# Feed-forward weights: split once and stored to scratch in the first row chunk, read back from there in the other three

## The chip, the core and the metric

The kernel runs on one core of a Trainium2 chip. The metric is the device time of one execution in microseconds (us), first to last: the median of three runs before the change is 1343.92 us.

## The reference

The output is a gated sum of two branches over the same 2048 rows of 512 values. Branch A is attention with 32 heads of 16 values that share one key and one value head. Branch B is a feed-forward network of width 1792. A gate per row, from `gate_w`, mixes them.

```python
g = sigmoid((x * gate_w).sum(-1, keepdims=True))
q = (x @ wq) per head; k = x @ wk; v = x @ wv
a = (softmax(q k^T * Dh**-0.5) @ v) over the heads @ wo
b = (silu(x @ w_gate) * (x @ w_up)) @ w_down
return g * a + (1 - g) * b
```

All inputs and the output are float32. Matmuls whose two sides would lose too much in one pass are made of three: each side is split into a rounded part (`h`, for high) and the rest (`l`, for low), and hh, hl and lh products are summed (`three`, L110).

## The kernel before, in words

**Preparation (L590 to L632).** x is loaded and transposed, and its two parts are kept for row chunks 0 and 1 (a chunk is 512 rows, there are four). Those of chunks 2 and 3 are stored to the scratch `x_d` and loaded again later. Keys, values and the gate are made, and the queries of the first 8 heads.

**Main loop (L771 to L815).** The order of every engine is written out by hand. For each head and each 128 keys, PE makes scores (`pss`, L660), ACT takes their exponentials (`pt`, L668; for some tiles DVE first copies half of the scores, L664), and PE sums them with the values (`po`, L680, in `mix`). From the 33rd group of keys on, four groups make one block (`block`, L711), which ends with four `mix` calls. Between the score matmuls, the block feeds matmuls of other jobs (`feed`, `Halves`, `Job.step` with L176): first the queries of the other 24 heads, then the feed-forward network. A job's 12 or 15 products run in two halves of 64 rows each: the low half first, the high half some steps later, after a one-element marker on DVE (`sign`, L403).

**Queries.** `query` (L198) leaves a job's result in `hh`, `hl` and, for the bound on the scores, in `hs` or `ht`; each is stored to the scratch `q_d` from SP (L232), where `load_head` (L640) reads the next head's queries into `qs`. The buffers: 7 for `hh`, 7 for `hl`, 2 each for `hs` and `ht`.

**Feed-forward.** For row chunk m and block f of 128 of the 1792 columns (14 of them), n = 14 m + f counts the steps. For every n there are three weight tiles of 128 x 512: g (`w_gate`), u (`w_up`) and d (`w_down`). In these texts g2 is the tile of `w_gate` for n = 2. `gate_up` makes the hidden values, `down` their product with `w_down`, summed over groups of four or five steps.

**The weights.** `load_w` (L144) calls `load_split` (L134). SP loads 256 KB into a raw buffer (`wraw`, L137; two of them, `WRB`), and GpSimd makes the two parts from it: a cast (L106) and a subtraction (L107). Each part of g and of u has two buffers, each part of d has five. So the splits of g and u for step n + 2 wait until PE has read those of step n. All four chunks need the same weights, so each tile is loaded and split four times. The loads for n = 0 and 1 and of the first five d tiles (L765 to L770) come before the loop; later ones of g and u are issued when a job of step n has ended (L309), those of d two at a time after jobs (L185). SP issues its DMAs in order, and waits at each until its buffer is free and its data is there. Among the weight loads stand the stores of `q_d`, of the attention output (`osb` to `o_d`, L694), and the loads of `qs`.

**Tail (L818 on).** When the attention is done, the remaining jobs run with all 128 rows at once, and `finish` (L432) multiplies the attention output, split by GpSimd from `o_d` (`load_o`, L424), with `wo`.

Of the kernel before, what the change touches and what calls it, by code (L numbers as in the profile page):

```python
# [8 lines left out]
F32 = mybir.dt.float32  # L9
F32R = mybir.dt.float32r  # L10
# [8 lines left out]
P = 128  # L19
S = 2048  # L20
D = 512
# [3 lines left out]
KD = D // P  # L25
NT = S // P
CH = 512
NCH = S // CH
TC = CH // P
NF = F // P  # L30
# [32 lines left out]
def tile_gated_mix(ctx, tc, x, wq, wk, wv, wo, w_gate, w_up, w_down, gate_w, out):  # L63
    nc = tc.nc
    x = x.rearrange("b s d -> (b s) d")
# [3 lines left out]
    dpool = ctx.enter_context(tc.tile_pool(name="dpool", bufs=1, space=DRAM))  # L69
# [5 lines left out]
    o_d = dpool.tile([D, S], F32, name="o_d")  # L75
    a_d = dpool.tile([NCH, P, TC, D], F32, name="a_d")
    x_d = dpool.tile([2, 2, P, KD, CH], F32, name="x_d")
    wq_v = wq.rearrange("(k p) n -> p k n", p=P)

    ident = cpool.tile([P, P], F32, name="ident")  # L80
# [20 lines left out]
    wp = tc.alloc_tile_pool(name="wp", bufs=2)  # L101
# [3 lines left out]
    def split(hi, lo, src, eng=nc.gpsimd, eng_hi=nc.vector):  # L105
        eng_hi.tensor_copy(hi, src)  # L106
        eng.tensor_tensor(lo, src, hi.bitcast(F32), ALU.subtract)  # L107
# [11 lines left out]
    wg_v = w_gate.rearrange("(k p) f -> p k f", p=P)  # L119
    wu_v = w_up.rearrange("(k p) f -> p k f", p=P)  # L120
    W, HT = {}, {}
    ACTS, DEFER, LOADS, HOLD, EVAC, FRESH = [], [], [], [], [], set()

    def run(queue, n):
        for _ in range(min(n, len(queue))):
            queue.pop(0)()
# [7 lines left out]
    def load_split(view, name, bufs, pool=wp):  # L134
        shape = list(view.shape)
        raw = wp.tile(shape, F32, name="wraw", bufs=WRB)
        nc.sync.dma_start(raw, view)  # L137
        hi = pool.tile(shape, F32R, name=name + "h", bufs=bufs)
        lo = pool.tile(shape, F32R, name=name + "l", bufs=bufs)
        split(hi, lo, raw, nc.gpsimd, nc.gpsimd)  # L140
        return hi, lo


    def load_w(nm, n):  # L144
        if n < NCH * NF:
            fs = slice(n % NF * P, (n % NF + 1) * P)
            if nm == "d":
                W[nm, n] = load_split(w_down[fs, :], "wd", 5)
            else:
                W[nm, n] = load_split({"g": wg_v, "u": wu_v}[nm][:, :, fs], "w" + nm, 2)  # L150

    def load_x_again(c):
        if c in ORDER:
# [99 lines left out]
    def gate_up(n, c):  # L253
# [53 lines left out]
        for nm, end in (("g", gate), ("u", up)):  # L307
            r.append(Job(3 * KD, lambda nm=nm: (nm, n) in W and c in XC, project(nm), end))
            r[-1].after.append(lambda nm=nm: load_w(nm, n + 2))  # L309
# [30 lines left out]
    def jobs():  # L340
        late = []
        for m, c in enumerate(ORDER):
            for fs in GROUPS:
                ns = [m * NF + f for f in fs]
                new = [job for n in ns for job in gate_up(n, c)]
                if late:
                    late[-1].after.append(lambda ns=ns: LOADS.extend([lambda n=n: load_w("d", n) for n in ns]))
                if fs[-1] == NF - 1:
                    if m < 2:
                        new[-1].after.append(lambda m=m: load_x_again(ORDER[m + 2]))  # L350
                for j, job in enumerate(new):
                    yield job
                    if late and j:
                        yield late.pop(0)
                yield from late
                late = [down(ns, c, i) for i in range(TC)]
            late[-1].after.append(lambda c=c: store_acc(c))
        yield from late
# [278 lines left out]
    with tc.tile_pool(name="bpool", bufs=2) as bp:  # L637
# [128 lines left out]
        for n in range(2):  # L766
            load_w("g", n)
            load_w("u", n)
        for n in GROUPS[0]:
            load_w("d", n)  # L770
        with tc.manual_schedule():  # L771
            for j in range(2):
                exps(*score(0, j))
            for n in range(BEGIN):
                quota = RATE
                u = 2 * n
# [20 lines left out]
            for k in range(2 * BEGIN // BLOCK, NB):  # L797
                u = BLOCK * k
                if k == 2 * BEGIN // BLOCK:
                    n = u + 6 - (u + 1)  # L800
# [129 lines left out]
```

## Time and profile before

| what | us |
|---|---|
| median of three runs (lowest, highest) | 1343.92 (1343.49, 1346.85) |
| the profiled execution | 1344.01 |
| its span, first to last instruction | 1341.9 |
| GpSimd: CAST and subtraction of the three weights, all 168 tiles | 36.1 + 36.1 + 35.1, 75.4 + 73.2 + 73.1 |
| DMA: moved in all | 107.79 MB, 80 GB/s on the mean |
| HBM | 76.09 MB read, 29.36 MB written |

PE is the matrix engine (PEld its weight loads), DVE the vector engine, ACT the scalar engine, POOL is GpSimd, and SP issues most of the DMAs. A row of the timeline has the start in us, the duration, the engine, the line of the kernel, the operation, what it writes and reads, how many instructions were merged, and in brackets the idle time before it and what ended it. A row of the waits has who waited for whom, the total in us, how often, and the longest. A row of the windows has a stretch, its length, the busy time of PE, PEld, DVE, ACT and POOL with instruction counts, the granted clock of PE as a share, the mean share of the 16 DMA engines, and GB/s.

### The profile page before, as it was taken

What the parts mean: (1) busy time and instruction counts of PE and PEld (TensorE: products, weight loads), DVE (VectorE), ACT (ScalarE), POOL (GpSimd) and SP (SyncE); (2) the same over time, 40 slices, a digit from 0 to 9 for tenths busy, and PEclk for the clock granted to TensorE, in tenths of its full rate; (3) what the DMA queues carried; (4) which work ended last, traced back from release to release, by engine and by line L of the source; (5) the groups of instructions that cost most, each with busy time, mean ns of one, the idle gap of its engine ahead of it and who ended that gap; (6) DMA issues with size and microseconds to landing.
All of it is one profiled execution on the core that took longest, in us unless ns stands there. A gap on an engine that the chain in (4) does not pass through costs nothing. (4 is left out here: it accounts for less than half of the span.)

```text
span 1341.9 us, 26802 instructions
## 1 busy us (share of the span) xinstructions
PE 1328.0 (99%) x10743; PEld 770.4 (57%) x10743; DVE 722.4 (54%) x1221; ACT 1061.6 (79%) x1463; POOL 391.0 (29%) x408
## 2 busy tenths in 40 slices
PE   9999999999999999999999999999999999999997
PEld 7655555555555555555555555555555555555576
DVE  5554565555455555555464555455454565465432
ACT  4578888888888888888888888888888888888400
POOL 6140321152042151152131241142131241333343
PEclk9999999999999999999999999999999999999999
DMA  8455221131122221141131221231121221222154
GB/s 277 142 173 190 65 60 38 35 107 44 44 86 77 78 80 38 35 107 44 52 122 39 82 79 39 57 83 45 52 61 30 81 79 39 74 68 60 44 161 143
DMA packets 101489, 107.79 MB, mean 80 GB/s; under 512 B 9968, under 2 KB 69616, under 8 KB 99696
## 3 DMA queue, kind: packets, MB, share of 16 engines
q1 hardware_dynamic: 99632, 105.81, 27.5%
q8 instruction: 88, 1.44, 0.5%
q10 hardware_dynamic: 1728, 0.20, 0.1%
q14 instruction: 41, 0.34, 0.1%
HBM read 76.09 MB, written 29.36 MB: 79 GB/s over the span
## 5 line engine op out<-in xcount | busy, mean ns | idle before, releaser
L668 ACT ACTIVATE pt<-pss 128x1024 f32<-128x1024 f32 (+1 forms) x1024 | 842.0, 876 | 177.3 <-PE pss L660 146.3
L664 DVE COPY pt<-pss 128x512 f32<-128x512 f32 x354 | 244.8, 692 | 415.6 <-PE pss L660 380.6
L680 PE MATMUL po<-pt,vaug 128*32 128x512 f32 x4096 | 467.6, 595 | 0.0
L660 PE MATMUL pss<-qs,ks 64*128 64x512 f32 x2048 | 403.1, 417 | 1.1 <-ACT pt L668 1.1
L660 PEld LDWEIGHTS pss<-qs,ks 64*128 64x128 f32 x2048 | 193.7, 184 | 218.4 <-ACT pt L668 183.6
L680 PEld LDWEIGHTS po<-pt,vaug 128*32 128x32 f32 x4096 | 119.2, 109 | 260.2 <-issue 255.2
L668 ACT ACTIVATE pt<-pt 128x512 f32<-128x512 f32 x354 | 195.7, 620 | 0.0
L176 PE MATMUL pf<-xh,wgl 64*128 64x512 f32 (+1 forms) x440 | 162.0, 392 | 0.0
L176 PE MATMUL pf<-xh,wgh 64*128 64x512 f32 (+1 forms) x440 | 160.5, 391 | 0.5 <-DVE acc L331 0.2
L176 PE MATMUL pf<-xl,wgh 64*128 64x512 f32 (+1 forms) x440 | 160.2, 390 | 0.0
L176 PE MATMUL pf<-xh,wuh 64*128 64x512 f32 (+1 forms) x440 | 158.4, 391 | 0.7 <-DVE sign L403 0.3
L176 PE MATMUL pf<-xl,wuh 64*128 64x512 f32 (+1 forms) x440 | 158.2, 390 | 0.0
L176 PE MATMUL pf<-xh,wul 64*128 64x512 f32 (+1 forms) x440 | 157.3, 391 | 0.0
L106 POOL CAST wgh<-wraw 128x512 fp32r<-128x512 f32 x56 | 36.1, 644 | 402.6 <-PE pf L176 311.8
L176 PE MATMUL pf<-wdh,hh 64*128 64x512 f32 (+1 forms) x427 | 143.4, 391 | 1.7 <-DVE hh L106 1.7
L176 PE MATMUL pf<-wdh,hl 64*128 64x512 f32 (+1 forms) x427 | 144.1, 390 | 0.0
L176 PE MATMUL pf<-wdl,hh 64*128 64x512 f32 (+1 forms) x427 | 143.4, 390 | 0.0
L689 DVE RECIPROCAL rsb<-rsb 128x128 f32<-128x128 f32 x128 | 117.1, 935 | 10.1 <-issue 8.2
L106 POOL CAST wuh<-wraw 128x512 fp32r<-128x512 f32 x56 | 35.1, 626 | 298.2 <-PE pf L176 245.3
L176 PEld LDWEIGHTS pf<-xh,wgh 64*128 64x128 f32 (+1 forms) x440 | 78.5, 185 | 9.8 <-issue 2.5
L176 PEld LDWEIGHTS pf<-xh,wuh 64*128 64x128 f32 (+1 forms) x440 | 77.3, 185 | 9.3 <-issue 3.7
L176 PEld LDWEIGHTS pf<-xl,wgh 64*128 64x128 f32 (+1 forms) x440 | 78.5, 185 | 6.0
(157 smaller groups left out, 1547.6 us busy)
## 6 DMA issues: line engine op xcount, KB each, us to landing
wraw<-in_B_w_gate_dram SPq DMA_DIRECT2D x56, 256.0 KB
wraw<-in_B_w_up_dram SPq DMA_DIRECT2D x56, 256.0 KB
wraw<-in_B_w_down_dram SPq DMA_DIRECT2D x56, 256.0 KB
qs<-q_d SPq DMA_DIRECT2D x62, 192.0 KB
q_d<-hl SPq DMA_DIRECT2D x18, 256.0 KB
q_d<-hh SPq DMA_DIRECT2D x18, 256.0 KB
o_d<-osb SPq DMA_DIRECT2D x128, 32.0 KB
a_d<-acc SPq DMA_DIRECT2D x4, 1024.0 KB
```

Of the source, the lines that this page charges most:

```text
L106: eng_hi.tensor_copy(hi, src)
L176: ins = nc.tensor.matmul(self.ps, a, b, start=(i == 0 and not half), stop=(last and half != 0))
L660: nc.tensor.matmul(ps[:, b * CH:(b + 1) * CH], ks[rows, kt * P:(kt + 1) * P], QS[h][rows, j, :], start=True, stop=True)
L664: other = nc.vector.tensor_copy(pt[:, CH:], ps[:, CH:]) if half else None
L668: ins = nc.scalar.activation(pt[:, w], ps[:, w], AF.Exp, scale=SCALE)
L680: nc.tensor.matmul(po[c * 2 * DH:(c + 1) * 2 * DH, :], vaug[:, kt, :], pt[:, c * CH:(c + 1) * CH], start=(kt == 0), stop=(kt == NT - 1))
L689: nc.vector.reciprocal(rsb[:, w], rsb[:, w])
```

## The change

In the first row chunk (n under 14) a tile is loaded and split as before. Then both parts are stored to a new scratch tensor `w_d` in HBM, 256 KB each. These stores are not issued at once: they are kept in `KEPT` and issued at the next call of `load_w`, right behind that call's own raw load. In the other three chunks nothing is split: after what is left in `KEPT`, SP loads the two parts from `w_d` into their buffers, with two DMAs of 256 KB. The other uses of `load_split` (`wq`, `wo`) are as before.

```diff
+    w_d = dpool.tile([3, NF, 2, P, D], F32, name="w_d")
...
+    KEPT = []
+
     def load_w(nm, n):
-        if n < NCH * NF:
-            fs = slice(n % NF * P, (n % NF + 1) * P)
-            if nm == "d":
-                W[nm, n] = load_split(w_down[fs, :], "wd", 5)
-            else:
-                W[nm, n] = load_split({"g": wg_v, "u": wu_v}[nm][:, :, fs], "w" + nm, 2)
+        if n >= NCH * NF:
+            return
+        f, bufs = n % NF, 5 if nm == "d" else 2
+        fs = slice(f * P, (f + 1) * P)
+        view = w_down[fs, :] if nm == "d" else {"g": wg_v, "u": wu_v}[nm][:, :, fs]
+        homes = [w_d["gud".index(nm), f, j] for j in range(2)]
+        if nm != "d":
+            homes = [home.rearrange("p (k f) -> p k f", k=KD) for home in homes]
+        if n < NF:
+            W[nm, n] = load_split(view, "w" + nm, bufs)
+            run(KEPT, len(KEPT))
+            KEPT.extend([lambda home=home, part=part: nc.sync.dma_start(home, part.bitcast(F32))
+                         for home, part in zip(homes, W[nm, n])])
+        else:
+            run(KEPT, len(KEPT))
+            W[nm, n] = [wp.tile(list(view.shape), F32R, name="w" + nm + x, bufs=bufs) for x in "hl"]
+            for home, part in zip(homes, W[nm, n]):
+                nc.sync.dma_start(part.bitcast(F32), home)
```

## The prediction

> **What bounds the kernel now.** I read the page's busy times first, then the waits, then the blocks of the attention loop, then DMA by stage.
>
> ```profile
> PE 1328.0 (99%) x10743; PEld 770.4 (57%) x10743; DVE 722.4 (54%) x1221; ACT 1061.6 (79%) x1463; POOL 391.0 (29%) x408
> ```
> ```profile
> POOL wgh L106 <- PE pf L176: 311.8, 39, 34.8
> POOL wuh L106 <- PE pf L176: 245.3, 40, 25.4
> ```
>
> PE is busy for 1328.0 of 1341.9 us; GpSimd, whose work the change takes away, for 391.0. Where GpSimd waits, it mostly waits for PE to let go of a weight buffer: it is ahead of PE, not behind. Busy time of matmuls is modelled, so I tested the bound on the loop's blocks. A block ends with four `mix` calls; it runs from one burst of `po` matmuls to the next.
>
> ```profile
> 392.57 0.64 PE L680 MATMUL po<-pt,vaug 128*32 128x512 f32 x4
> ...
> 1214.56 0.64 PE L680 MATMUL po<-pt,vaug 128*32 128x512 f32 x4
> 1223.95 0.64 PE L680 MATMUL po<-pt,vaug 128*32 128x512 f32 x4
> 1233.31 0.64 PE L680 MATMUL po<-pt,vaug 128*32 128x512 f32 x4
> 1242.72 0.64 PE L680 MATMUL po<-pt,vaug 128*32 128x512 f32 x4
> ```
> ```profile
> 1214.56:1223.95 9.39, 9.39 (x83) 5.36 (x81) 5.40 (x8) 8.46 (x14) 6.90 (x8) 1.00 0.32 90
> 1233.31:1242.72 9.41, 9.41 (x83) 5.38 (x81) 5.99 (x11) 7.96 (x13) 0.00 (x0) 1.00 0.10 28
> ```
>
> In the windows GpSimd's busy time stands before the clock. The block with 6.90 us of splits took 9.39 us, the one with none 9.41. So in the loop PE sets the pace, and the splits cost it next to nothing. From 392.57 to 1242.72 lie 90 blocks, 9.45 us on average.
>
> The one long stage where another resource is full is the beginning, in which the queries are made and stored to `q_d`:
>
> ```profile
> 18.00:28.00 10.00, 10.00 (x58) 8.20 (x57) 5.46 (x8) 4.68 (x9) 8.52 (x10) 1.00 0.95 385
> 46.00:72.00 26.00, 26.00 (x191) 15.23 (x191) 12.64 (x23) 18.62 (x20) 1.91 (x2) 1.00 0.55 200
> 74.00:99.00 25.00, 25.00 (x208) 12.97 (x200) 14.14 (x25) 19.23 (x21) 13.63 (x14) 1.00 0.58 172
> 101.00:136.00 35.00, 34.05 (x272) 17.60 (x269) 16.44 (x32) 29.05 (x32) 2.46 (x3) 1.00 0.60 192
> 390.00:1252.00 862.00, 861.02 (x7267) 484.78 (x7265) 478.39 (x812) 746.81 (x1046) 237.20 (x245) 1.00 0.24 64
> ```
>
> The last two columns are the DMA engines' share and GB/s. From 18 to 28, where `x_d` is stored, the engines are full at 385 GB/s. From 46 to 136 the share never passes 0.60, yet the rate sticks near 200 GB/s: the `q_d` stores seem to fill about half of the engines and leave the others idle. After 390 the share is 0.24.
>
> **The change, part by part.**
>
> *Start: the new stores.* The loads g0, u0, g1, u1, d0 to d4 are all issued inside this stage. Now each is followed by two 256 KB stores, held back until the next load has been issued. So the stores of eight loads, 16 in all, enter SP's queue before the load of g2; those of d4 come just behind it.
>
> ```profile
> 81.03 0.38 SPq L137 DMA_DIRECT2D wraw<-in_B_w_gate_dram  x1
> ...
> 99.14 0.33 SPq L137 DMA_DIRECT2D wraw<-in_B_w_down_dram  x1
> 100.83 0.60 SPq L232 DMA_DIRECT2D q_d<-ht  x1
> 129.66 0.60 SPq L232 DMA_DIRECT2D q_d<-ht  x1
> 130.53 1.03 SPq L137 DMA_DIRECT2D wraw<-in_B_w_gate_dram  x1
> ```
> ```profile
> 78.28 0.69 DVE L222 SCALAR_TENSOR_TENSOR ht<-ht 128x512 fp32r<-128x512 f32 x1
> ...
> 107.72 0.49 DVE L221 TENSOR_SCALAR ht<-hh,kmax 128x512 f32<-128x512 f32 x1 [0.63 <-DMA q_d<-ht]
> ```
> ```profile
> 137.96 0.77 POOL L106 CAST wgh<-wraw 128x512 fp32r<-128x512 f32 x1 [34.24 <-DMA wraw<-in_B_w_gate_dram]
> 138.81 1.60 POOL L107 TENSOR_TENSOR wgl<-wraw,wgh 128x512 fp32r<-128x512 f32 x1
> ```
> ```profile
> 142.42 0.39 PE L176 MATMUL pf<-xh,wgh 64*128 64x512 f32 x1
> ```
>
> This chain has no room. The raw load of g2 was issued at 130.53 and landed at 137.96, its split ended at 140.41, and the first matmul on it (counted in program order) ran at 142.42: 2.0 us of slack. At 107.72 DVE even waited for a `q_d` store, and it was SP that was late: that buffer was filled at 79, and its store was issued at 100.83, behind the raw loads that wait for splits.
>
> The price of a store has two rows. At the `q_d` pace (200 GB/s) 256 KB take 1.31 us, 16 of them 21.0; at the `x_d` pace (385) 0.68, in all 10.9. I take the second: `x_d`'s stores too have all 128 partitions as their outer dimension, `q_d`'s have 8 heads. The Trainium skill, "DMA: Bandwidth & Descriptors", section "Why a DMA increments its semaphore by 16 and not by 1", says that the outermost dimension sets how many of the 16 engines a DMA uses, so 8 for `q_d`; the shares of 0.55 and 0.95 agree, and by that rule the sum is the 10.9.
>
> From this go the pauses in which SP waited for splits. The stage 74 to 99 moved 172 GB/s where 46 to 72 moved 200: 25 x (1 - 172/200) = 3.5 us idle. The splits that made the pauses remain, and each store waits for one, so I credit half, 1.8. SP is then 10.9 - 1.8 = 9.1 us late behind 99, and from there to 130 it issues `q_d` stores at the DMA's pace and catches up nothing. Queued behind it are the `q_d` stores, whose buffers DVE reuses, head 2's `qs`, and g2: whoever stops PE first, the total is the lateness less the smallest slack, 9.1 - 2.0 = **+7.1 us**. Ends: all absorbed by idle engines, 0; the `q_d` price without credit, +19.0.
>
> *First row chunk, later loads.* Each load's stores sit ahead of the raw load after the next. The chunk's tight place is u9:
>
> ```profile
> 277.58 0.38 SPq L137 DMA_DIRECT2D wraw<-in_B_w_up_dram  x1
> ```
> ```profile
> 281.19 1.28 POOL L107 TENSOR_TENSOR wul<-wraw,wuh 128x512 fp32r<-128x512 f32 x1
> ```
> ```profile
> 285.03 0.39 PE L176 MATMUL pf<-xh,wuh 64*128 64x512 f32 x1
> ```
>
> Split done at 282.47, used at 285.03: 2.6 us of slack. Two stores ahead cost two issues of 0.4 and 1.4 us of transfer, 2.2. It just fits; the loads right behind it build up the same delay, so I put **+0.3** (ends 0 and 2).
>
> *Chunks 1 to 3: no split, two direct loads.* 126 splits leave GpSimd, each a cast of 0.61 us and a subtraction of 1.3 (rows below and above): 241 us. A direct load must wait on SP until PE releases the buffer, where the raw load went ahead into `wraw`. Queued behind it on SP are `osb` stores and the next head's `qs`, issued a head ahead. What counts is release to next use:
>
> ```profile
> 1096.19 0.61 POOL L106 CAST wuh<-wraw 128x512 fp32r<-128x512 f32 x1 [5.98 <-PE pf L176]
> ```
> ```profile
> 1105.77 0.39 PE L176 MATMUL pf<-xh,wuh 64*128 64x512 f32 x1
> ```
> ```profile
> 1267.00 7.58 SPq L137 DMA_DIRECT2D wraw<-in_B_w_down_dram  x4
> ```
> ```profile
> 1269.79 0.61 POOL L106 CAST wdh<-wraw 128x512 fp32r<-128x512 f32 x1 [0.49 <-DMA wraw<-in_B_w_down_dram]
> ```
>
> This buffer was free at 1096.2 and used at 1105.8: 9.6 us, about the least of these chunks when I match buffers to matmuls in program order. One 256 KB load lands 2.8 us after its issue; the second adds 0.4 of issue and 0.7 of transfer: 3.9. Six us stay, so **0**; the cover is gone when a pair takes over 9.6 us. The traffic of a chunk doubles, on engines with a share of 0.24. DVE's two-input operations run beside no split any more; on PE I give that **-0.4**, near the two blocks' difference of nothing (ends 0 and -5.0, if all 90 blocks fell from 9.45 to 9.39).
>
> *Tail.* Here PE does wait for DVE, and DVE runs beside the splits of d52 to d55:
>
> ```profile
> 1278.76 0.39 PE L176 MATMUL pf<-wdl,hh 128*128 128x512 f32 x1
> 1278.98 0.39 PE L176 MATMUL pf<-wdh,hl 128*128 128x512 f32 x1
> 1281.03 0.47 PE L176 MATMUL pf<-wdh,hh 128*128 128x512 f32 x1 [1.66 <-DVE hh L106]
> ```
> ```profile
> 1273.11 1.66 DVE L107 TENSOR_TENSOR hl<-ht,hh 128x512 fp32r<-128x512 f32 x1
> ...
> 1275.68 1.49 DVE L692 TENSOR_TENSOR osb<-osb,rsb 128x512 f32<-128x512 f32 x1
> 1277.09 0.68 DVE L266 COPY hs<-pf 128x512 f32<-128x512 f32 x1
> 1278.46 1.17 DVE L284 SCALAR_TENSOR_TENSOR ht<-ht,hs 128x512 f32<-128x512 f32 x1 [0.70 <-ACT ht L276]
> ...
> 1280.92 0.69 DVE L107 TENSOR_TENSOR hl<-ht,hh 128x512 fp32r<-128x512 f32 x1
> ```
>
> The same L107 takes 0.69 us alone and 1.66 beside a split; L692 and L284 are 0.8 and 0.5 over that 0.69, together 2.3 on the way to 1281.03. The step from one of PE's matmuls to the next is 0.22, so its stall is 2.05 - 0.22 = 1.8, and all of it goes: **-1.8**. The eight direct loads (8 x 0.68 = 5.4 us from 1267, and 2.8) are there by about 1275, before PE's stop at 1279.
>
> *Sum.* The profiled execution took 1344.01 us, 0.1 over the median. 1344.0 + 7.1 + 0.3 - 0.4 - 1.8 = 1349.2, so **1349.1** on the median.
>
> **Rivals.**
>
> *The stores are absorbed.* They use the idle half of the engines and the pauses, and g2 is not late. For it: shares of 0.55 to 0.60. Against: 2.0 us of slack and a DVE already waiting. It holds if the lateness stays under 2.0. Time: 1344.0 - 1.8 - 0.4 = 1341.8.
>
> *Direct loads come late.* Doubled transfers meet `osb`, `qs` and the reload of x, and a pair takes over 9.6 us. At 0.4 us each on the some 30 loads with so short a time: +12 on the forecast, 1361. Against: the share of 0.24.
>
> *The splits cost DVE, and so PE, more than the blocks show.* All 90 blocks fall to 9.39 and the start costs nothing: 1344.0 - 1.8 - 5.0 = 1337.2. The mechanism is the stretched L107. The Trainium skill, "SBUF — State Buffer", section "Who interferes with whom", calls the port pair that the two engines share an exclusive lock; the 1.66 beside 0.69 agrees. Against: 9.39 beside 9.41.
>
> *The change moves work that nobody waited for*, in the tail and start too: 1344.
>
> **How the numbers follow.** About 0.3% (4 us) is what a measurement of this kernel can tell from no change. Forecast 0.60, of which 0.08 lie under 1347.9 (a start loss under 6); absorbed 0.22 (0.20 within 0.3%, 0.02 faster); late loads 0.10; DVE 0.05, faster; nothing 0.03. So slower 0.52 + 0.10 = 0.62, within 0.31, faster 0.07. The range, 1341 to 1356, takes in the absorbed case and a start loss of up to 14, and leaves out the late loads, the DVE case and the rest of the `q_d` price, under 0.2.
>
> **What would show it.** After the change GpSimd should be busy some 241 us less, near 150. Right: a PE gap of several us between 107 and 150, DVE waiting for `q_d` stores near 110 for several us instead of 0.63, g2's cast later than 138 beside its use; no gap of 2 us before the last `down` jobs; blocks after 390 unchanged. Wrong: PE without a gap before 150, or waits of PE on DMA in the later chunks.

## The result, and the profile after

The changed kernel takes 1354.0 us (median of six runs, 1352.9 to 1355.7); the kernel before, beside it on the same chip, 1345.4 (six runs, 1343.5 to 1347.1). The ratio is 1.0067, with a 95% interval of 1.0052 to 1.0081: slower, by 0.7%. The profiled execution took 1352.9 us, its span 1350.8, 8.9 more than the span of before.

Busy times on the page of the changed kernel:

```profile
PE 1329.6 (98%) x10743; PEld 770.8 (57%) x10743; DVE 701.8 (52%) x1221; ACT 1061.9 (79%) x1463; POOL 144.3 (11%) x156
```

GpSimd lost 246.7 us of work (391.0 before), and PE is busy for 1.6 us more. Where the time went is read from the same bursts of `po` matmuls in both kernels. Timeline of PE, first before, then after:

```profile
82.64 0.64 PE L680 MATMUL po<-pt,vaug 128*32 128x512 f32 x4
156.25 0.64 PE L680 MATMUL po<-pt,vaug 128*32 128x512 f32 x4
1259.14 0.64 PE L680 MATMUL po<-pt,vaug 128*32 128x512 f32 x4
```
```profile
82.57 0.64 PE L695 MATMUL po<-pt,vaug 128*32 128x512 f32 x4
167.65 0.64 PE L695 MATMUL po<-pt,vaug 128*32 128x512 f32 x4
403.89 0.64 PE L695 MATMUL po<-pt,vaug 128*32 128x512 f32 x4
1270.09 0.64 PE L695 MATMUL po<-pt,vaug 128*32 128x512 f32 x4
```

Up to 82 the two run alike. Between the bursts at 82 and 156 the changed kernel loses 11.5 us, up to the last burst it gains 0.5 back (11.40 to 10.95), and from there to the end of the span it is 2.0 us shorter: 11.5 - 0.5 - 2.0, less the 0.1 by which it was ahead at 82, is 8.9. The whole loss lies in some 75 us. I use the bursts of 82, 156 and 1259 for every experiment below (start, loop, tail), since executions already differ by -0.1 to 1.4 us ahead of the first of them.

In that stretch PE stands once. PE's timeline of the changed kernel, and one of the waits from 80 to 130:

```profile
99.64 0.39 PE L191 MATMUL pf<-xl,wq3h 64*128 64x512 f32 x1
108.83 0.79 PE L191 MATMUL pf<-xh,wq3h 64*128 64x512 f32 x1 [8.79 <-DVE sign L418]
```
```profile
DVE ht L236 <- DMA q_d<-ht: 13.5, 1, 13.5
```

PE waits for `sign`, the little memset with which DVE marks the end of a half job. DVE has not come to it, because an instruction ahead of it on DVE waits 13.5 us for a `q_d<-ht` store. DVE's timeline:

```profile
105.96 0.49 DVE L236 TENSOR_SCALAR ht<-hh,kmax 128x512 f32<-128x512 f32 x1 [13.53 <-DMA q_d<-ht]
...
108.69 0.06 DVE L418 MEMSET sign<- 1x1 f32 x1
```

`ht` has two buffers. The one wanted at 92.4 was filled four jobs earlier, and its store is the third of the trio `hl`, `hh`, `ht` that SP issues near 77. SP's timeline of before, with the last two of the trio together (the last row is needed further below):

```profile
76.11 0.65 SPq L232 DMA_DIRECT2D q_d<-hh  x1
76.86 0.60 SPq L232 DMA_DIRECT2D q_d<-ht  x1
...
114.16 1.18 SPq L645 DMA_DIRECT2D qs<-q_d  x1
```

After the change the trio is torn apart:

```profile
76.96 0.64 SPq L247 DMA_DIRECT2D q_d<-hh  x1
...
99.33 0.38 SPq L138 DMA_DIRECT2D wraw<-in_B_w_down_dram  x1
...
101.39 0.32 SPq L159 DMA_DIRECT2D w_d<-wdl  x1
101.81 0.61 SPq L247 DMA_DIRECT2D q_d<-ht  x1
...
121.39 1.22 SPq L660 DMA_DIRECT2D qs<-q_d  x1
...
137.94 1.32 SPq L138 DMA_DIRECT2D wraw<-in_B_w_gate_dram  x1
```

The third store went from 76.86 to 101.81, behind seven raw loads and sixteen `w_d` stores. Each of those waits its turn for a split on GpSimd, so SP does not pass them faster than GpSimd splits. The order of SP's instructions is fixed when the kernel is built: the loads, and now their stores, stand in the code ahead of the queries. In the kernel before, six `q_d` stores were still placed between the first of these loads and the last; in the changed one two were, and the rest came behind them all. Why the placing came out so is not shown; the rows show that it did.

Fourteen of the sixteen stores took SP next to no time. Windows from 80 to 101, before and after (the last two columns are the DMA engines' share and GB/s):

```profile
80.00:101.00 21.00, 21.00 (x176) 11.62 (x174) 12.92 (x22) 16.47 (x18) 14.65 (x15) 1.00 0.48 146
```
```profile
80.00:101.00 21.00, 20.03 (x165) 10.74 (x161) 6.08 (x12) 16.50 (x18) 14.47 (x16) 1.00 0.83 271
```

They went through engines that were idle before, and the last raw load of the stage, which stands behind these fourteen, went out at 99.33 where it was at 99.14. What is late stands behind it. From there to the load of head 2's `qs` SP issued 12 `q_d` stores before; now it issues 16 of them and two `w_d` stores, and takes 22.1 us (99.33 to 121.39) in place of 15.0 (99.14 to 114.16), 1.2 for each of the six.

One more thing is in the rows: after the stop PE runs slowly. Windows of the changed kernel (granted clock third from the right):

```profile
103.00:104.00 1.00, 0.00 (x0) 0.00 (x0) 0.00 (x0) 0.00 (x0) 1.00 (x1) 0.75 0.53 76
110.00:112.00 2.00, 2.00 (x14) 1.53 (x12) 1.17 (x3) 0.00 (x0) 0.00 (x0) 0.50 0.53 203
113.00:114.00 1.00, 1.00 (x8) 0.20 (x9) 1.00 (x3) 0.80 (x2) 0.00 (x0) 0.63 0.53 201
114.00:115.00 1.00, 1.00 (x16) 0.24 (x8) 0.55 (x1) 0.52 (x1) 0.00 (x0) 1.00 0.53 205
```

Some 3.6 us into the stop the granted clock falls to 0.50, and it stays there until about 113.7 (0.63 is the mean of the window from 113 to 114), 4.9 us after PE has gone on. That costs half of 4.9. So the 11.5 us are 9.0 of standing (a step of 9.19 less the usual 0.22) and 2.5 at half clock. The Trainium skill, "TensorE: Matmul & The Clock Gate", section "What's actually happening", gives about 3.4 us of idling for the fall to half clock and as much work for the way back; the 3.6 and 4.9 here are near that.

And the tail: where a step of PE took 2.05 us before, the steps are now even. PE's timeline of the changed kernel:

```profile
1289.93 0.39 PE L191 MATMUL pf<-wdh,hl 128*128 128x512 f32 x1
1290.15 0.39 PE L191 MATMUL pf<-wdh,hh 128*128 128x512 f32 x1
```

### The profile page after: what moved, and what is told of

It reads as the page before. It is cut to its first block, busy times and chain, and to the rows that moved or that the text cites. A ratio compares the mean times of both kernels' runs of the same rounds, so it can differ in the third digit from the quotient of the medians.

```text
span 1350.8 us, 26678 instructions
## 1 busy us (share of the span) xinstructions
PE 1329.6 (98%) x10743; PEld 770.8 (57%) x10743; DVE 701.8 (52%) x1221; ACT 1061.9 (79%) x1463; POOL 144.3 (11%) x156
## 5 line engine op out<-in xcount | busy, mean ns | idle before, releaser
L107 POOL CAST xh<-wraw 128x512 fp32r<-128x512 f32 x16 | 10.3, 641 | 855.5 <-DMA wraw<-o_d 855.5
L191 PEld LDWEIGHTS pf<-xh,wgl 64*128 64x128 f32 (+1 forms) x440 | 78.5, 185 | 5.7
```

The lines of the kernel that those rows point to most:

```text
L191: ins = nc.tensor.matmul(self.ps, a, b, start=(i == 0 and not half), stop=(last and half != 0))
```

## The experiments

"Start" is what a run loses against before's profile between the bursts at 82 and 156, "loop" from there to 1259, "tail" from there to the end of the span; medians and ratios are those of all timed runs against the kernel before on the same chip (1345.4 to 1347.0 there).

| run | start | loop | tail | median us | ratio, 95% |
|---|---|---|---|---|---|
| the change | +11.5 | -0.5 | -2.0 | 1354.0 | 1.0067 [1.0052, 1.0081] |
| e4_store_only | +12.7 | +0.8 | -0.5 | 1358.6 | 1.0102 [1.0085, 1.0119] |
| e2_gpsimd_queue | +5.9 | -1.0 | -1.8 | 1350.3 | 1.0036 [1.0022, 1.0051] |
| e1_spread | +17.3 | -1.0 | -2.0 | 1359.4 | 1.0098 [1.0079, 1.0118] |
| e10_rings | +8.2 | -0.8 | -2.2 | 1351.8 | 1.0049 [1.0031, 1.0067] |
| e8_fill | +9.6 | -0.4 | -1.9 | 1351.9 | 1.0042 [1.0027, 1.0056] |
| e5_tail | +11.8 | -0.4 | +0.2 | 1357.7 | 1.0089 [1.0069, 1.0108] |
| e6_late | 0.0 | +5.1 | -2.5 | 1348.5 | 1.0012 [0.9999, 1.0024] |
| e3_nine | 0.0 | -0.6 | -2.7 | 1341.2 | 0.9967 [0.9954, 0.9979] |
| e7_four | 0.0 | -0.2 | -3.2 | 1341.6 | 0.9965 [0.9953, 0.9978] |
| e9_dlate | 0.0 | -0.9 | -1.3 | 1341.8 | 0.9967 [0.9956, 0.9977] |
| e11_before | 0.0 | -0.2 | +0.3 | 1344.2 (one run) | |
| e12_tail_fill | 0.0 | -0.3 | +0.4 | 1344.7 | 0.9991 [0.9983, 1.0000] |

**Is the loss all in the stores of the start?** The stores alone, without the direct loads:

```diff
-            W[nm, n] = [wp.tile(list(view.shape), F32R, name="w" + nm + x, bufs=bufs) for x in "hl"]
-            for home, part in zip(homes, W[nm, n]):
-                nc.sync.dma_start(part.bitcast(F32), home)
+            W[nm, n] = load_split(view, "w" + nm, bufs)
```

> The kernel before with all 84 stores to w_d of the first chunk as in the changed kernel, but every later chunk loads the raw weights and splits them as before; nobody reads w_d. Theory START (the whole loss is made by the stores ahead of 124 us: 9.0 us of PE standing and 2.4 us of half clock; the direct loads give 0.4 and the tail 2.0 back): 1345.4 + 11.4 = 1356.8, 1355.5 to 1358, with PE's step of about 9 us near 100 and the 2.0 us step ahead of the last down jobs still there. Rival DIRECT (the direct loads cost some of the 8.6): under 1354.

Its start loses 12.7 us in the same place, by the same wait, and its tail is as long as before's to 0.5 us. One of its waits from 80 to 130:

```profile
DVE ht L234 <- DMA q_d<-ht: 14.5, 1, 14.5
```

START stands, though the median is 0.6 above its range; DIRECT falls: the reads from scratch cost nothing that can be seen.

**The other way round:** no stores for g0, u0, g1, u1, d0 to d4, which the later chunks split again.

```diff
-        if n < NF:
+        if n < NF or f < bufs:
             W[nm, n] = load_split(view, "w" + nm, bufs)
             run(KEPT, len(KEPT))
+            if f < bufs:
+                return
```

> The changed kernel without the stores of the first nine loads (g0, u0, g1, u1, d0 to d4); the later chunks split these nine again and read the other 33 parts of a chunk from scratch. Nothing is stored to w_d before g2. Both theories of the start, ORDER and VOLUME: PE's step at 99.64 is gone, time at the blocks as in the kernel before, then -0.4 in the loop and -2.0 in the tail (d52 to d55 are read from scratch here too): 1345.4 - 2.4 = 1343.0, 1342 to 1344.5. Rival DIRECT (part of the loss is made by direct loads or by the stores of the rest of the first chunk): 1346 or more.

The start loses nothing. The median gains even 5 us, more than the 3.3 of the profile in loop and tail, and lies under the 1342 to 1344.5 foretold; to that I come back with the last run.

**Order or volume?** The same transfers in the same stage, but the `w_d` stores on GpSimd's own queue, so that SP keeps its old order:

```diff
-            KEPT.extend([lambda home=home, part=part: nc.sync.dma_start(home, part.bitcast(F32))
+            KEPT.extend([lambda home=home, part=part: nc.gpsimd.dma_start(home, part.bitcast(F32))
```

> The changed kernel with the stores to w_d issued from GpSimd's own DMA queue; SP keeps the order of instructions that it has in the kernel before. Same transfers in the same stage. Theory ORDER (the loss at the start comes from the place of one q_d<-ht store, which in SP's queue fell behind seven raw loads and sixteen w_d stores, so that DVE waited 13.5 us for its buffer): that store is back near 77 us, the wait of DVE for q_d<-ht is under 2 us, the 9.2 us step of PE at 99.64 is gone, and with the tail (-2.0) and the loop (-0.4) the time is 1343 to 1346 us. Rival VOLUME (4.5 MB more through engines that are busy in this stage, wherever they are issued; the term of the prediction): g2 is still 7 us late and PE stops for about 5 to 7 us somewhere between 107 and 150: 1349 to 1354.

Each is half right: PE's step at 99.64 is gone, as ORDER said, but 5.9 us are lost, and the median lies in VOLUME's range. SP's timeline, DVE's, and PE's two stops:

```profile
79.25 0.87 SPq L247 DMA_DIRECT2D q_d<-ht  x1
...
105.72 1.62 SPq L247 DMA_DIRECT2D q_d<-ht  x1
...
139.48 1.25 SPq L138 DMA_DIRECT2D wraw<-in_B_w_gate_dram  x1
```
```profile
115.03 0.49 DVE L236 TENSOR_SCALAR ht<-hh,kmax 128x512 f32<-128x512 f32 x1 [6.99 <-DMA q_d<-ht]
```
```profile
117.90 0.50 PE L191 MATMUL pf<-xh,wq3h 64*128 64x512 f32 x1 [2.25 <-DVE sign L418]
...
136.15 0.50 PE L675 MATMUL pss<-qs,ks 64*128 64x512 f32 x2 [1.73 <-ACT pt L683]
```

The store of 77 is in its old place, and DVE does not wait at 92. But the next `ht` store, issued at 105.72, took 9.3 us until DVE could write again (6.9 before, 100.83 to 107.72), and g2's load went out at 139.48 where it was at 130.53; less the 0.9 us by which this execution began late, 8.1 late. Less g2's slack of 2.0 that makes 6.1, next to the 5.9 measured, but g2 stopped nobody: its split ended at 149.6, and no wait of PE is on it. PE lost 4.4 us at its first stop, behind the `ht` wait, with the half clock after it (windows in the last section), and 1.5 at the second, where ACT itself had waited 1.3 us for a `q_d<-ht` store.

Nor are the 5.9 the price of the volume alone. GpSimd issues its stores itself in this run, some 0.55 us each between its splits, and the raw loads wait for those splits: the last of them went out at 103.93, 3.9 us late, where in the changed kernel it was 0.2 late. So with SP's order held half of the loss goes; what the same transfers would cost with the splits undisturbed stays open.

**Same queue, same stage, other order.** Two stores per step from the sixth step of the stage on, so that `q_d<-ht` keeps its place:

```diff
             W[nm, n] = load_split(view, "w" + nm, bufs)
-            run(KEPT, len(KEPT))
+            if n >= bufs:
+                run(KEPT, len(KEPT))
...
                 settle()
+                if n >= 5:
+                    run(KEPT, 2)
                 mix(u)
```

> The changed kernel with the first 18 stores to w_d still on SP's queue and in the same stage, but written two per step into the loop of the first 16 pairs of key tiles, from the sixth on, so that SP's queue holds them between the q_d stores and the q_d<-ht store of 77 us stays ahead of the raw loads. Theory ORDER+VOLUME (of the 11.4 us at the start some 6 are the volume, as the run with GpSimd's queue lost 5.9, and some 5.5 the place of that one store): PE has no step near 100; g2 and the q_d stores become late little by little, PE loses 5 to 8 us by 150: 1348 to 1351. Rival QUEUE (only a second queue helps, on SP the loss stays): 11 us or more by 150, 1354 or above.

There is no step near 100, as ORDER+VOLUME said, but 17.3 us are lost, far over its 5 to 8. The bound of QUEUE is met, though its reason, that only a second queue helps, falls with two runs that issue all 84 stores on SP without a loss at the start (e6_late and e9_dlate below). SP's timeline and PE's waits from 120 to 160:

```profile
102.18 0.73 SPq L248 DMA_DIRECT2D q_d<-ht  x1
102.96 1.58 SPq L160 DMA_DIRECT2D w_d<-wgh  x1
...
127.78 1.25 SPq L661 DMA_DIRECT2D qs<-q_d  x1
```
```profile
PE pss L676 <- DMA qs<-q_d: 7.4, 2, 7.0
PE pf L192 <- POOL wgh L107: 2.8, 1, 2.8
```

Here the stores stand where SP has no pauses. Ahead of the load of head 2's `qs` are ten of them; that load is 127.78 - 0.9 - 114.2 = 12.7 us later than before, 1.3 per store. That is the `q_d` pace, the price that the prediction did not take. In the changed kernel sixteen stores stand ahead of g2's load, among the splits, and that load is 7.4 us later (137.94 for 130.53): 0.5 each on the average, next to nothing for the fourteen ahead of the last raw load and 1.2 for each store more behind it. What a store costs SP depends on what SP waits for around it.

The second wait is one on g2's split, the stop that the prediction had in mind. With the half clock behind it, it makes 4.9 of the 17.3.

**Fewer of them in front.** The full change, with d0 to d4 loaded behind u2:

```diff
-        for n in GROUPS[0]:
-            load_w("d", n)
...
+                if ns[0] == 0:
+                    new[5].after.append(lambda: LOADS.extend([lambda n=n: load_w("d", n) for n in GROUPS[0]]))
```

> The changed kernel, all 42 parts stored and read again, but d0 to d4 are loaded (and so stored) only behind the up job of u2 in place of ahead of the queries: of the first 18 stores six stay ahead of the q_d stores, and so do four raw loads in place of nine. Theory QUEUE PLACE (PE's 9.0 us are q_d stores that stand on SP behind loads that wait for splits and behind their stores): the store of 77 us is issued near 89 in place of 101.8, DVE waits under 2.5 us for it, PE has no step over 1 us near 100 and the granted clock stays at 1.00; 0 to 2 us at the start, then -0.4 and -2.0 (tail): 1354.0 - 11.4 + 1 = 1343.6. Rival VOLUME (each early store costs its 0.68 us, six cost 4.1 less the slack of 2.0; and the twelve moved ones make the loads of the first groups late): 1346 to 1350.

The start loses 0.0. SP's and DVE's timelines:

```profile
87.91 0.61 SPq L247 DMA_DIRECT2D q_d<-ht  x1
```
```profile
92.31 0.48 DVE L236 TENSOR_SCALAR ht<-hh,kmax 128x512 f32<-128x512 f32 x1
```

The store of 77 still stands behind two raw loads and six `w_d` stores, yet at 87.91 it is early enough and DVE does not wait at all. All 84 stores are made and all 252 loads of the later chunks come from scratch, and the kernel is faster than before, 0.9967. QUEUE PLACE stands, and VOLUME's 1346 to 1350 does not. But the run moves volume as well as order: with five raw loads and ten stores out of the way, g2's load goes out at 123.97, 6.6 us earlier than before.

**Does the buffer decide?** With the third part of a query in the rings of seven buffers:

```diff
-            if m:
-                qb = wp.tile([P, CH], F32, name="ht" if c % 2 else "hs", bufs=2)
-                nc.vector.tensor_copy(qh, ps)
-            else:
-                qb = wp.tile([P, CH], F32R, name="hl" if c % 2 else "hh", bufs=7).bitcast(F32)
+            qb = wp.tile([P, CH], F32R, name="hl" if c % 2 else "hh", bufs=7).bitcast(F32)
+            if m:
+                nc.vector.tensor_copy(qh, ps)
+            else:
```

> The changed kernel, but the third part of each query (hs, ht: two buffers each) is written into the rings of hh and hl with seven buffers each, as in the first 128 columns already. Loads, stores and SP's order as in the changed kernel. Theory BUFFER (DVE waits because the buffer that it wants to fill at 92.4 is that of a store issued at 101.8): with the rings the first buffer whose store is late comes a job later, near 98; DVE's wait is 8 to 11 us in place of 13.5 and starts there, PE loses 5 to 8 us in place of 11.4 up to 150: 1348 to 1351. Rival PACE (what counts is when the q_d stores are through, whatever the buffers): 11 us as before, 1354.

DVE's timeline:

```profile
106.83 0.69 DVE L233 TENSOR_TENSOR hl<-pf,hh 128x512 fp32r<-128x512 f32 x1 [8.26 <-DMA q_d<-hl]
109.81 0.48 DVE L235 TENSOR_SCALAR hh<-hh,kmax 128x512 f32<-128x512 f32 x1 [2.29 <-DMA q_d<-hh]
```

The wait starts a job later, near 98.6, and lasts 8.3 and 2.3 us; the start loses 8.2, just over the 8 that BUFFER allowed, as the median is (1351.8 for 1351). More buffers move the wait back by a job; they do not bring the stores forward.

**The half clock.** 40 matmuls of no use ahead of the one that waits:

```diff
+FILL = 40
...
+        job.query = (m, c)
...
+                if i == 0 and getattr(job, "query", None) == (3, 0):
+                    pz = ps_s.tile([P, 2 * CH], F32, name="pss")
+                    for _ in range(FILL):
+                        nc.tensor.matmul(pz[:, :CH], ks[:RT, :P], ks[:RT, :CH], start=True, stop=True)
```

> The changed kernel with 40 matmuls of no use (64x128 by 64x512, into a score buffer that nobody reads) put on PE just ahead of the matmul that waits at 99.64 us; they take about 9 us, as long as the wait. Theory CLOCK (2.4 of the 11.4 us are matmuls run at the half clock that was granted after PE had stood): the granted clock stays at 1.00 from 100 to 120, the blocks are 9.0 us late instead of 11.4, in all 1354.0 - 2.4 = 1351.6. Rival NO CLOCK (the 2.4 us are late data too, and the records only show it as clock): 11.4 us late as before, 1354 or above.

Windows, with the clock third from the right; the second is 0.84 in the changed kernel:

```profile
99.00:109.00 10.00, 10.00 (x79) 5.41 (x78) 2.35 (x4) 5.72 (x6) 4.03 (x5) 1.00 0.67 214
109.00:124.00 15.00, 14.95 (x122) 7.80 (x121) 11.74 (x21) 11.47 (x12) 0.00 (x0) 1.00 0.52 199
```

The wait of DVE is 13.9 us, near the 13.5 of the changed kernel; the start loses 9.6 in place of 11.5, where CLOCK had 9.0. The median is 2.1 lower than the changed kernel's, or 3.7 when each is set against the kernel before beside it. CLOCK stands.

**Stores behind g2.** Each pair goes out only with the load that takes over its buffer:

```diff
+            raw = wp.tile(list(view.shape), F32, name="wraw", bufs=WRB)
+            nc.sync.dma_start(raw, view)
+        for home, part in KEPT.pop((nm, n - bufs), ()):
+            nc.sync.dma_start(home, part.bitcast(F32))
```

> The changed kernel with each pair of stores issued only by the load that takes over its buffer, behind the raw load and ahead of the split. All 84 stores are made, but none ahead of g2's raw load; 18 of them follow in the stage from 130 us on. ORDER: all is as in the kernel before up to 130; g2's cast now also waits for the landing of two stores issued 1 to 2 us behind its raw load, 0 to 1.5 us of its 2.0 us of slack: no PE step over 1 us before 160, 1343 to 1345. Rival VOLUME (18 stores cost 7 us at least wherever they stand in a stage whose share is near 0.6): 1348 to 1353.

The start is free, as ORDER had it, but the loop is 5.1 us longer: 1.4 go near 305 and 4.7 near 485, where g19's direct load comes out behind direct loads and late stores of down parts and an `osb` store, and 1.0 comes back elsewhere. So the median, 1348.5, lies in VOLUME's range, but the loss is not where VOLUME put it. One of the waits from 470 to 500:

```profile
PE pf L193 <- DMA wgh<-w_d: 2.8, 1, 2.8
```

This is the rival "direct loads come late" of the prediction, on one load: the change itself does not have it, a version that stores later does.

**The tail.** First the last four parts split again, then only d10 to d13 kept, for the last chunk alone:

```diff
+        if nm == "d" and n >= NCH * NF - 4:
+            W[nm, n] = load_split(view, "w" + nm, bufs)
```
```diff
-        if n < NF:
+        if nm != "d" or f < 10 or n < (NCH - 1) * NF:
             W[nm, n] = load_split(view, "w" + nm, bufs)
             run(KEPT, len(KEPT))
+            if nm != "d" or f < 10 or n >= NF:
+                return
```

> The changed kernel with the last four down parts (d52 to d55) loaded raw and split on GpSimd again. Theory SPLIT (PE's stop of 1.8 us ahead of the last down jobs is made by those splits beside DVE): the step of about 2.0 us is back near 1290, the tail is 1.8 to 2.0 us longer than in the changed kernel, 1355.9. Rival TRAFFIC (the stop went because of other things in the tail, as the place of the loads on SP): no such step, 1354.0.

> Only four of the 42 parts are stored (d10 to d13, behind 150 us) and read again, in the last chunk alone; all others are split as in the kernel before. Theory SPLIT: the start is that of the kernel before, the loop does not change, the tail is 2.0 us shorter: 1343.5 where the kernel before has 1345.4 to 1346.2. Rival LOOP (the version with 33 parts read from scratch is 5 us faster by the medians because 99 splits fewer pay in the loop, and the tail is only a part): its blocks then show that gain and this one does not, 1344 to 1345 here against 1341.

In the first the stop is back; PE's timeline:

```profile
1290.51 0.39 PE L193 MATMUL pf<-wdh,hl 128*128 128x512 f32 x1
1292.65 0.47 PE L193 MATMUL pf<-wdh,hh 128*128 128x512 f32 x1 [1.75 <-DVE hh L107]
```

In the second four parts, each stored once and read once, bring as much as the 33 of e3_nine, 1341.6 beside 1341.2 (ratios 0.9965 and 0.9967). SPLIT stands, though the medians lie 1.8 above and 1.9 below what it said, and LOOP falls: 99 splits fewer in the loop are worth half a microsecond at most, where the kernel before, run again, differs by 0.2 from itself.

Of the tails of -1.3 to -3.2 in the table, 1.8 lie at the stop itself, in the change as in e3_nine, e7_four and e9_dlate. The rest lies behind 1314, where PE waits for GpSimd's splits of `o_d`; there the kernel before, run again (e11_before), is itself 0.6 longer.

**Why the medians give more than the profiles.** The three versions without the tail's stop and without a loss (e3_nine, e7_four, e9_dlate) gain 4.2 to 5.4 us by the medians, 2.0 to 3.2 by the spans of the profiles. One more profile of before, unchanged:

> The kernel before, once more, for its profile alone: its times lie between 1343.5 and 1349.2, and the profile of before is of one of its shorter executions. Theory TAIL (the executions differ in the length of PE's stop ahead of the last down jobs, which is why the medians give the versions without that stop more than the 2.0 us of the profile): an execution of 1346 us has the same blocks up to 1259 and a stop of over 3 us. Rival HEAD (they differ ahead of the loop, by the 0 to 1.4 us that the first blocks of the runs differ by): the stop is 2.0 us and the blocks are later from the first on.

It drew an execution of 1344.2, one of the shorter ones, with a stop of 1.98: nothing is decided by it. Then before with the stop filled:

```diff
+FILL = 8
...
+            if i == getattr(self, "pad", None):
+                pz = ps_s.tile([P, 2 * CH], F32, name="pss")
+                for _ in range(FILL):
+                    nc.tensor.matmul(pz[:, :CH], ks[:RT, :P], ks[:RT, :CH], start=True, stop=True)
...
+        late[0].pad = 9
```

> The kernel before with 8 matmuls of no use (64x128 by 64x512, 0.22 us each) on PE where it stands for 1.8 us ahead of the last down jobs; the wait for DVE itself stays. In the profiles the tail without the splits of d52 to d55 is worth 2.0 us, in the medians of the versions with and without them 3.7 to 5. Theory CLOCK (in some executions the short stop is followed by a stretch at half clock, so the stop costs 2 us in the shorter ones and 4 to 5 in the others): with PE kept busy the longer executions go, times of 1343.5 to 1345.5, median 1344, where the kernel before spreads from 1343.5 to 1349. Rival WAIT (the executions differ in something else): median 1346 and the same spread.

PE's timeline; the useless matmuls end where the data come:

```profile
1279.87 2.11 PE L175 MATMUL pss<-ks 64*128 64x512 f32 x8
1281.91 0.50 PE L181 MATMUL pf<-wdh,hh 128*128 128x512 f32 x1
```

The wait is as long, but twelve executions lie between 1343.8 and 1345.7, where seventeen of before lie between 1343.3 and 1349.7, and the median is 1.1 lower. That is what CLOCK foretold, with a median of 1344.7 for 1344. The mean granted clock of each execution points the same way. Of the 59 executions of before beside the experiments, 26 have a mean clock of 0.999 and take 1344.8 us on the mean, 26 have 0.998 and take 1346.9, three have 0.996 and take 1349.3; all twelve with the stop filled, and all of e7_four and e9_dlate, have 0.999 or more. So the longer executions do run longer at half clock. That it stands behind the tail's stop is argued; no profile of such an execution was at hand.

## Why the prediction was right, and where its sum was off

The direction and the kind of loss were right: slower, with DVE waiting for a `q_d` store and PE for DVE, by 8.9 us in the profiles where +5.2 was forecast. The place was near: PE's gap lies at 100 to 109 and not between 107 and 150. That the time fell into the range is luck in part, since what made most of the loss was not in the sum. Point by point:

- **Start, +7.1: measured +11.5.** Two steps failed: "SP is then 10.9 - 1.8 = 9.1 us late behind 99", and "whoever stops PE first, the total is the lateness less the smallest slack, 9.1 - 2.0". Both took SP's order of before as kept and only moved everything back. Behind 99 SP was 0.2 us late; the 7.4 by which g2's load went out late grew behind that, by six more stores, four of them `q_d` stores out of their place. And g2 stopped nobody. Its split came late, and PE even later; GpSimd's and PE's timelines:

```profile
144.90 0.61 POOL L107 CAST wgh<-wraw 128x512 fp32r<-128x512 f32 x1 [40.80 <-DMA wraw<-in_B_w_gate_dram]
145.59 1.29 POOL L108 TENSOR_TENSOR wgl<-wraw,wgh 128x512 fp32r<-128x512 f32 x1
```
```profile
153.57 0.62 PE L191 MATMUL pf<-xh,wgh 64*128 64x512 f32 x2
```

  The split ended at 146.9, and the first matmul on it, the second of these two, ran at 153.8. What stopped PE was one `q_d` store that changed its place by 25 us. With the order held (e2_gpsimd_queue) the formula gives 6.1 and the chip 5.9, but by other stops than g2's and with half clock in it: that is luck. In e1_spread g2 did stop PE.
- **Half clock: not in the sum, 2.5.** The prediction priced a stop at its length.
- **Price of a store.** 0.68 was taken, of two rows. On SP it was next to nothing among the splits and 1.2 to 1.3 between `q_d` stores. The ends of the range, 0 and 19, held both.
- **First chunk, +0.3: -0.1** (the 11.4 at 156 are 11.3 at the burst of 403.89, which stood at 392.57 before).
- **Direct loads, 0: 0.** PE waits for no direct load in the changed kernel; SP does the waiting, 366.8 us on PE's feed-forward matmuls, as the prediction had it. From SP's own waits:

```profile
SPq L165 <- PE pf L191: 366.8, 83, 17.8
```

- **Loop, -0.4: -0.4** from there on, and -0.2 to -1.0 in the other versions with fewer splits, e6_late with its late stores apart. The kernel before, run again, has -0.2, so little of this is clear of the differences between executions.
- **Tail, -1.8: -2.0** in the profile, 1.8 of it at the stop, by the splits beside DVE, as said (e5_tail, e7_four). By the medians of e5_tail and the change, 1357.7 and 1354.0, it is 3.7; but when each is set against the kernel before beside it (1347.0 and 1345.4), it is 2.0.

The sum with the measured terms: 1344.0 + 11.5 - 0.1 - 0.4 - 2.0 = 1353.0, where the profiled execution took 1352.9 (it was 0.07 ahead at 82). Of the rivals, "absorbed" had the right reason for the stretch from 80 to 101, idle engines and pauses, but not the order behind it; it would have been right for six early stores in place of sixteen, with five raw loads moved too (e9_dlate). "Direct loads late" would have been right for stores behind their loads (e6_late).

## What to carry to other kernels

Before you price an added transfer, find what will stand behind it on its queue, one instruction at a time: a store that guards a buffer of an in-order engine may be worth more than all the bytes that you add, and an instruction added early in the code can push it back by 25 us, as here. Put additions into stretches in which the queue waits anyhow, few at a time, and look again at the queue's order after the edit. And ask first which splits anybody waited for: here four of 126.

## What the runs showed of the hardware

A stop of PE can cost more than its length. After 9.0 us the clock was 0.50 for 4.9 us more. But much shorter stops were enough too: in e2_gpsimd_queue PE stood from 115.5 to 117.9 and from 134.3 to 136.2, for 2.4 and 1.9 us, and windows behind these stops read

```profile
118.00:120.00 2.00, 2.00 (x16) 1.66 (x18) 1.13 (x2) 0.00 (x0) 0.00 (x0) 0.86 0.52 178
121.00:122.00 1.00, 1.00 (x5) 0.20 (x8) 0.93 (x3) 0.81 (x2) 0.00 (x0) 0.50 0.52 195
137.00:138.00 1.00, 1.00 (x8) 0.84 (x6) 0.28 (x1) 0.95 (x3) 0.00 (x0) 0.50 0.61 197
```

Half clock for some 3.4 us each time, and that after PE was at work again; in e1_spread another stop of 1.9 us, from 140.7 to 142.5, was followed by the same. The section of the Trainium skill named above asks for an idle window of about 3.4 us; these stops were shorter, so here the measurement decides. A stop of 1.8 us (the tail of before) left the clock at 1.00 in both profiles. The stretches at half clock lasted 3.4 us behind these three stops, 6.8 in e10_rings (109.7 to 116.6) and 10.2 in the changed kernel (103.5 to 113.7).
